# Re-spacing the w_sp sums, adding b_sp on VectorE alone, and one lo part moved ahead at the start, in an FNet and gMLP block on one core

## The chip, the cores and the metric

The kernel runs on one core of a Trainium2 chip. The metric is the device time of one execution in microseconds. The kernel before took 965.06 us (median of 3 runs, 964.96 to 966.77). The profile is that of one further execution.

## The reference

Two layers stand one behind the other, each scaled, shifted and gated by rows of a modulation vector. The first is a Fourier mixing of the sequence, the second a gated MLP whose gate mixes the sequence with w_sp and adds b_sp:

```python
mod = (_silu(c) @ w_mod).reshape(c.shape[0], 6, 1, -1)
sa, ca, ga, sb, cb, gb = (mod[:, i] for i in range(6))
h = _layernorm(x) * (1 + ca) + sa
a, b = h @ dft_hid_re.T, h @ dft_hid_im.T
x = x + ga * (dft_seq_re @ a - dft_seq_im @ b)
h = _layernorm(x) * (1 + cb) + sb
z = _gelu(h @ w_in)                          # 2048 x 1792
z1, z2 = z[..., :896], _layernorm(z[..., 896:])
g = w_sp @ z2 + b_sp[:, None]                # w_sp is 2048 x 2048
x = x + gb * ((z1 * g) @ w_out)
```

The sequence has 2048 rows, the hidden size is 512, all in fp32.

## The kernel before

**Products in three matmuls.** Each fp32 operand is split into a hi part, rounded to fp32r by ScalarE (`ah`, `hh`, `gh`, `bh`), and a lo part, the rest, made by VectorE (`al`, `hl`, `gl`, `bl`). A product is hi x hi, hi x lo and lo x hi (`matmul3`, L95 to L97).

**Chunks.** The program is a long row of chunks of matmuls on TensorE. Chunk n has one 128 x 512 strip as its moving or weight operand, and up to 12 matmuls. Chunks 0 to 127 are the products with the sequence DFT matrices (`gp`, `mm_a`); in between stand the products with the hidden DFT (`yp`, `mm_y`). `N2` = 128 and `N3` = 144 begin the two halves of w_in (`z1p`, `z2p`), `N4` = 160 the product with w_sp (`gw`, `mm_w`), which ends with chunk 271. The tail (`op`) multiplies with w_out.

**Preparing a chunk.** A block of 512 x 512 comes from DRAM into a `stage` tile (two buffers, four DMAs on SyncE's queue, L151 or L157). VectorE transposes it, two chunks at a time, into `t` (`turn_two`, L204 or L210), ScalarE makes `ah`, VectorE makes `al`. `prep(n)` issues al of chunk n+2 (three buffers, so it waits until chunk n-1 is through on TensorE), on even n the pair of chunks n+4 and n+5, and ah of chunk n+3. The turn of a block's second pair frees its stage, and SyncE then loads the block after the next.

**What sets the order.** The order on each engine is that in which the program issues: `at(n, f, ...)` puts a piece of work behind chunk n's matmuls, `run(n)` issues what was put there. Each engine and each DMA queue takes its own work strictly in this order.

**w_sp in seven products.** The product with w_sp is done in quadrants, by a scheme with seven products (`PROD` = 1, 6, 7, 4, 5, 3, 2, of 16 chunks each, beginning at `NB[p]`) instead of eight. Four of them need sums and differences of w_sp's quadrants. These are made ahead: `load_s` loads a unit (two DMAs on SyncE's queue, L602, 1 MB into a tile `sj`), `sum_s` makes two of the four sums, then two more (VectorE, L607 to L612), and each result goes to DRAM by a DMA on GpSimd's queue (L615). Eight units fall in chunks 90 to 122, through two buffers in a pool `spre0` that takes the memory of the pool of the modulation rows (`change_q`, which so has to follow the last use of modulation row 5); eight more units come later.

**Modulation row 5.** `load_mod` loads it, `sum_mod` sums it in four steps on VectorE (L268, L270), `split_mod` splits it, `spread_mod` spreads it by two matmuls.

**The gate.** `keep_w` copies the product's banks out of PSUM into tiles `g` (ScalarE, L672). `add_bs` adds b_sp (L689): on GpSimd for `p` = 4 and 7, on VectorE for 1 and 6. `make_u` multiplies with z1 (VectorE, L698), `add_w` adds later products into g (VectorE, L678).

**The start.** The first four chunks go through L413, with hh and hl of the first four rows of h in turn: all four matmuls of hi x hi, then lo x hi, then hi x lo. `lo_h` makes hl (L394).

Of the kernel before, what the change touches and what calls it, by code (L numbers as in the profile page):

```python
# [10 lines left out]
AF = mybir.ActivationFunctionType  # L11
ALU = mybir.AluOpType
# [7 lines left out]
def fnet_gmlp_kernel(  # L20
# [32 lines left out]
    nc = tc.nc  # L53
# [69 lines left out]
    def at(n, f, *a):  # L123
        fill.setdefault(n, []).append((f, a))
# [14 lines left out]
    N2 = 4 * len(src)  # L139
# [5 lines left out]
    NB = {p: N4 + 4 * NQ * i for i, p in enumerate(PROD)}  # L145
# [31 lines left out]
    def prep(n):  # L177

        if n not in prepared:
            prepared.add(n)  # L180
            prep_lo(n + 2)
            if n % 2 == 0:
                turn_two(n + 4)
            prep_hi(n + 3)

# [9 lines left out]
    def turn_two(n):  # L195

        if n >= NE:
            return
        b, k = divmod(n, 4)
        st = stage[b]  # L200
        t = blocks.tile([P, 2, Q], F32, tag="t", bufs=2, name=f"t{n}")
        T[n], T[n + 1] = t[:, 0, :], t[:, 1, :]
        if n >= N4:
            nc.vector.transpose(t.rearrange("p r (b i) -> p r b i", i=32), st[:, :, :, 16 * k:16 * k + 32])  # L204
        elif n >= N3:
            for m in range(2):
                nc.vector.transpose(T[n + m].rearrange("p (k a i) -> p a k i", k=4, i=32),
                                    st[:, :, 32 * (k + m):32 * (k + m) + 32].rearrange("p (a k) i -> p a k i", k=4))
        else:
            nc.vector.transpose(t.rearrange("p k (b i) -> p k b i", i=32),  # L210
                                st[:, :, 32 * k:32 * k + 64].rearrange("p b (k i) -> p k b i", k=2))
        if k == 2:
            stage.pop(b)
            load(b + 2)

    def prep_hi(n, eng=None):
        if n >= NE:
            return
        AH[n] = blocks.tile([P, Q], F32R, tag="ah", bufs=4, name=f"ah{n}")
        if eng:  # L220
            eng.tensor_scalar(AH[n], T[n], 1.0, None, op0=ALU.mult)
        else:
            nc.scalar.activation(AH[n], T[n], AF.Copy)  # L223

    def prep_lo(n):
        if n >= NE:
            return
        AL[n] = blocks.tile([P, Q], F32R, tag="al", bufs=3, name=f"al{n}")
        nc.vector.tensor_tensor(AL[n], T.pop(n), AH[n].bitcast(F32), op=ALU.subtract)  # L229
# [388 lines left out]
    GW, UT, X2, OP, G, BH, BL = {}, {}, {}, {}, {}, {}, {}  # L618
    wo_hi, wo_lo, wor, Z1T = {}, {}, {}, {}
# [24 lines left out]
    def mm_w(n):  # L644
        i, m = divmod(n - N4, 4 * NQ)
        p, k, r = PROD[i], m // 2, m % 2
        nf = 4 if p in (1, 6, 4, 2) else 3
        fresh = p in (1, 5, 2)
        if k == 0 and fresh:
            for f in range(nf):  # L650
                k_ = 4 * r + f if p == 1 else 3 * r + f if p == 5 else (6, 7, 0, 1, 2, 3, 4, 5)[4 * r + f]
                GW[r, f] = bank(k_, f"gw{p}_{r}_{f}")
        ah, al = AH.pop(n), AL.pop(n)
        for f in range(nf):
            cols = slice(f * P, (f + 1) * P)
            matmul3(GW[r, f], BH[p, k][:, cols], BL[p, k][:, cols], ah, al, fresh and k == 0, k == 7, not fresh)
        if k == 7:
            if p in (1, 6, 7, 4):
                keep_w(p, r)
            elif p != 2:  # L660
                add_w(p, r, range(3))
            else:
                add_w(p, r, range(2 if r == 0 else 0))

    def keep_w(p, r):

        if p in (1, 4):
            G[p, r] = spre[-1].tile([P, 4, Q], F32, tag="sj", bufs=4, name=f"g{p}_{r}")
        else:
            G[p, r] = gpool[0].tile([P, 3, Q], F32, name=f"g{p}_{r}")  # L670
        for f in range(G[p, r].shape[1]):
            nc.scalar.activation(G[p, r][:, f, :], GW[r, f], AF.Copy)  # L672

    def add_w(p, r, fs):

# [9 lines left out]

    def add_bs(p, r, f):
        g = G[p, r][:, f, :]
        eng, b = (nc.vector, r) if p in (1, 6) else (nc.gpsimd, 2 + r)
        eng.tensor_tensor(g, g, wor["bs", b], op=ALU.add)  # L689

    def load_z1(p, r):
        f0, f1 = (0, 4) if p in (1, 4) else (4, NF)
# [100 lines left out]
    load(2)  # L793
    at(0, lo_h, 2)
    at(0, hi_h, 3)
    at(1, lo_h, 3)
    at(0, load_x, 1, range(2, 4))
    at(2, load_row)
# [7 lines left out]
    for s, n in ((4, 4), (5, 4), (6, 6), (7, 6), (8, 10), (9, 10)):  # L806
        m = n + (s == 9)
# [23 lines left out]
    for j, turn, weigh, row, fold, hi in ((0, (25, 26, 27, 28), (29, 29, 30, 30), 26, (34, 34, 35, 36), (38, 35, 36, 37)),  # L831
# [8 lines left out]
        n = weigh[3] + (3 if j == 0 else 1)  # L840
# [4 lines left out]
            at(hi[k], make_ht, j, k)  # L845
            at(hi[k] + 1, make_ht_lo, j, k)
    for j, load_at, n, m, k, plus_one in ((2, 41, 49, 50, 7, False), (4, 52, 56, 58, 7, True),
                                          (3, 60, 65, 66, 7, False), (5, 68, 85, 86, 6, False)):
        at(load_at, load_mod, j)
        at(n, sum_mod, j, [0, 1])  # L850
        at(m, sum_mod, j, [2, 3])
        at(m + 1, split_mod, j)
        at(m + 3, spread_mod, j, k, cpool if j == 5 else htpool, plus_one)
    for t in range(NQ):
        n = 8 * NQ * (t + 1)
        for i in range(4):
            y = N2 - 1 if t == NQ - 1 else (54, 56, 58, 60)[i] if t == 0 else n + (7, 9, 11, 13)[i] if t == 1 else n + 1 + 3 * i
            if i < 2:
                at(y - 4, load_xr, t, i)
            if t == 0:  # L860
                at((41, 42, 43, 45)[i], mm_y, t, i, (0,))
                at((42, 43, 44, 46)[i], keep_y, t, i)
            at(y, mm_y, t, i, (0, 1) if t else (1,))
            if t < NQ - 1:
                at(y + 1, post_y, t, i)
                at(y + 2, norm_y, t, i)
                at(y + 3 if t else 71 + i, post_h, t, i)
                if i < 2:
                    at(y + 2 if t else y + 3, load_xr, t, i + 2)
            else:  # L870
                if i > 1:
                    at(N2 - 0.25, prep, N2 + i - 2)
                at(N2 - 0.25, post_y, t, i)
                at(N2 - 0.25, norm_y, t, i)
                at(N2 - 0.25, post_h, t, i)
                if i < 2:
                    at(N2 - 0.25, load_xr, t, i + 2)
                for k in ((0,), (1,), (2, 3), ())[i]:
                    at(N2 - 0.25, make_wi, 0, k)
                    at(N2 - 0.25, make_wi_lo, 0, k)  # L880
# [25 lines left out]
        hq.close()  # L906
        spre.append(hp.enter_context(pool("spre0")))

    at(90, change_q)
    at(N2 + 3, change_s)  # L910
    for i, u in enumerate((r, g, b) for g in range(2) for b in range(4) for r in range(2)):
        n = 90 + 4 * i if i < 8 else N2 + 6 + 3 * (i - 8)
        at(n, load_s, *u)
        at(n + 3, sum_s, *u, True)
        at(n + 4, sum_s, *u, False)
    for n in range(N2):
        prep(n)
        mm_a(n)
        run(n)
        run(n + 0.5)  # L920
        run(n + 0.75)
# [6 lines left out]
    for n in range(N2, N3):  # L928
        prep(n)
        run(n)  # L930
        two_first(mm_z1, n, n - N2, ND)
# [8 lines left out]
    for i, p in enumerate(PROD):  # L940
        for k in range(8):
            n = NB[p] + 2 * k
# [25 lines left out]
    at(N4 + 4, change_g)  # L968
    at(NB[3] + 1, change_o)
    for r in range(2):  # L970
        for f in range(4):
            at(NB[5] + 2 + 8 * r + 2 * f, add_bs, 4, r, f)
            if f < 3:
                at(NB[4] + 2 + 3 * r + f, add_bs, 7, r, f)
    at(NB[3] + 3, load_z1, 4, 0)
    at(NB[3] + 4, load_z1, 7, 0)
    for f in range(4):
        at(NB[2] + 3 + f, make_u, 4, 0, f)
        if f < 3:
            at(NB[2] + 7 + f, make_u, 7, 0, f)  # L980
    at(NB[2] + 8, load_z1, 4, 1)
    at(NB[2] + 11, load_z1, 7, 1)
    for f in range(NF):
        n = NB[6] + 3 * f
# [2 lines left out]
        at(n - 2, make_wo, f)  # L987
        at(n - 1, make_wo_lo, f)
    order = [(t, i) for t in (2, 3, 0, 1) for i in range(4)]
    later = {0: [(make_u, 4, 1, 0), (make_u, 4, 1, 1), (add_w, 2, 0, [2])],  # L990
             1: [(make_u, 4, 1, 2), (make_u, 4, 1, 3), (add_w, 2, 0, [3]), (load_z1, 1, 0)],
             2: [(make_u, 7, 1, 0), (make_u, 7, 1, 1), (make_u, 7, 1, 2), (load_z1, 6, 0)],
             3: [(add_w, 2, 1, [0, 1])], 4: [(add_w, 2, 1, [2, 3])]}
    for n, p, r in ((3, 1, 0), (5, 6, 0), (7, 1, 1), (9, 6, 1)):
        for f in range(4 if p == 1 else 3):
            later.setdefault(n + f // 2, []).extend([(add_bs, p, r, f), (make_u, p, r, f)])
# [53 lines left out]
```

## Time and profile before

| | us |
|---|---|
| median of 3 runs | 965.06 |
| the profiled execution | 966.28 |
| its span in the trace | 964.5 |
| TensorE busy | 950.2 |
| VectorE busy | 674.4 |
| ScalarE busy | 366.6 |
| GpSimd busy | 188.7 |
| mean granted clock of TensorE | 0.997 |

Times in the trace count from the span's start. A row of the order of time has start, length, engine, line of the kernel, operation, out<-in, shapes and count; what stands in brackets is how long the engine stood idle just before, and for whom. Matmuls overlap, so their pace is read from start to start. A row of waits has the total, how often, and the longest. A row of windows has, for each of TensorE, its weight loads, VectorE, ScalarE and GpSimd, the busy time and the count, then the granted clock, the DMA engines' share and GB/s. SPq, ACTq and POOLq are queues that issue DMAs.

### The profile page before, as it was taken

Reading aid. Unit: us, or ns where it says so; the run is one execution under the profiler, and the core shown is the slowest. Engines: PE = TensorE matmul, PEld = TensorE weight load, DVE = VectorE, ACT = ScalarE, POOL = GpSimd, SP = SyncE. Lnnn points to the kernel's source line nnn. Section 1 sums busy time; section 2 is a strip of 40 time slices with the busy share of each in tenths; the row PEclk is TensorE's granted clock in tenths of the full one; section 3 lists DMA queues with packets and bytes.
Section 4 is the critical chain, followed back from the end, with each engine's and each line's share of the span. In section 5 each row is a group of like instructions: output and inputs, shape, how many; then the busy total and the mean of one; then the engine's idle time right before and its main releaser. Section 6 shows DMA issues by size and latency. Waiting matters only on the chain.

```text
span 964.5 us, 12252 instructions
## 1 busy us (share of the span) xinstructions
PE 950.2 (99%) x4196; PEld 789.6 (82%) x4196; DVE 674.4 (70%) x980; ACT 366.6 (38%) x631; POOL 188.7 (20%) x342
## 2 busy tenths in 40 slices
PE   8999999999999999989999999999999999999998
PEld 5888888888888888768888999888887888888886
DVE  6799857675465768556536477878689688775882
ACT  4684424232222223122433446635544354432221
POOL 1330000222520254113413344200004050000000
PEclk9999999999999999999999999999999999999999
DMA  9996654566455787787398864555555355933541
GB/s 211 219 222 139 118 128 100 150 164 164 131 132 130 200 265 229 234 234 171 129 293 300 296 215 153 135 138 128 138 120 116 90 131 118 217 94 119 194 161 60
DMA packets 249535, 161.27 MB, mean 167 GB/s; under 512 B 130176, under 2 KB 218240, under 8 KB 249344
## 3 DMA queue, kind: packets, MB, share of 16 engines
q1 hardware_dynamic: 236800, 122.72, 52.5%
q0 software_dynamic: 11424, 37.24, 10.7%
q8 instruction: 33, 0.54, 0.2%
q10 hardware_dynamic: 1248, 0.52, 0.2%
q14 instruction: 30, 0.25, 0.1%
HBM read 123.73 MB, written 36.70 MB: 166 GB/s over the span
## 4 chain that ended last, share of the span: by engine, by line
PE 88%; DMA 6%; DVE 3%; SPq 2%; issue 1%; DVEq 0%; ACTq 0%
PE gp L96 10%; PE gp L97 10%; PE gp L95 10%; PE gw L96 9%; PE gw L95 9%; PE gw L97 9%; DMA sj<-in_B_w_sp_dram 4%; PE z2p L96 3%; PE z2p L97 3%; PE z2p L95 3%; PE op L97 3%; PE z1p L96 3%; PE op L96 3%; PE z1p L95 3%; PE yp L96 3%; PE yp L95 3%
## 5 line engine op out<-in xcount | busy, mean ns | idle before, releaser
L223 ACT ACTIVATE ah<-t 128x512 fp32r<-128x512 f32 x271 | 169.5, 628 | 355.7 <-PE gp L97 164.2
L229 DVE TENSOR_TENSOR al<-t,ah 128x512 fp32r<-128x512 f32 x272 | 193.0, 715 | 155.4 <-PE gp L96 54.9
L96 PE MATMUL gp<-al,hh 128*128 128x512 f32 x496 | 194.1, 391 | 4.5 <-DVE al L229 4.4
L97 PE MATMUL gp<-ah,hl 128*128 128x512 f32 x496 | 193.9, 391 | 0.0
L95 PE MATMUL gp<-ah,hh 128*128 128x512 f32 x496 | 193.9, 391 | 0.0
L96 PE MATMUL gw<-al,bh 128*128 128x512 f32 x400 | 155.9, 390 | 1.4 <-DVE al L229 1.4
L95 PE MATMUL gw<-ah,bh 128*128 128x512 f32 x400 | 155.8, 390 | 0.0
L97 PE MATMUL gw<-ah,bl 128*128 128x512 f32 x400 | 155.8, 390 | 0.0
L96 PEld LDWEIGHTS gp<-al,hh 128*128 128x128 f32 x496 | 93.5, 189 | 25.1 <-DVE al L229 5.7
L95 PEld LDWEIGHTS gp<-ah,hh 128*128 128x128 f32 x496 | 93.6, 189 | 19.5
L97 PEld LDWEIGHTS gp<-ah,hl 128*128 128x128 f32 x496 | 93.4, 188 | 19.4
L210 DVE STREAM_TRANSPOSE t<-stage 128x1024 f32<-128x1024 f32 x70 | 86.7, 1239 | 4.3 <-DMA stage<-in_A_dft_seq_re_dram 3.2
L96 PEld LDWEIGHTS gw<-al,bh 128*128 128x128 f32 x400 | 75.1, 188 | 17.3 <-DVE al L229 1.8
L95 PEld LDWEIGHTS gw<-ah,bh 128*128 128x128 f32 x400 | 75.1, 188 | 15.6
L97 PEld LDWEIGHTS gw<-ah,bl 128*128 128x128 f32 x400 | 75.1, 188 | 15.6
L204 DVE STREAM_TRANSPOSE t<-stage 128x1024 f32<-128x1024 f32 x56 | 69.4, 1238 | 0.9 <-DMA stage<-in_B_w_sp_dram 0.9
L615 POOL DMA_DIRECT2D s_d<-sj x64 | 35.3, 551 | 144.6 <-DVE sj L607 109.2
L637 ACT ACTIVATE bh<-z 128x512 fp32r<-128x512 f32 (+1 forms) x56 | 32.8, 586 | 59.8 <-PE gw L96 55.5
L689 POOL TENSOR_TENSOR g<-g,bs 128x512 f32<-128x512 f32 x14 | 22.5, 1644 | 141.1 <-ACT g L672 141.1
L95 PE MATMUL yp<-hth,gh 128*128 128x512 f32 x128 | 49.9, 389 | 0.0
L97 PE MATMUL yp<-hth,gl 128*128 128x512 f32 x128 | 49.9, 389 | 0.0
L96 PE MATMUL yp<-htl,gh 128*128 128x512 f32 x128 | 49.9, 389 | 0.0
(152 smaller groups left out, 1398.4 us busy)
## 6 DMA issues: line engine op xcount, KB each, us to landing
stage<-in_A_dft_seq_im_dram SPq DMA_DIRECT2D x64, 256.0 KB, 5.5
sj<-in_B_w_sp_dram SPq DMA_DIRECT2D x32, 512.0 KB, 7.5
s_d<-sj POOLq DMA_DIRECT2D x64, 256.0 KB, 4.2
stage<-s_d SPq DMA_DIRECT2D x128, 128.0 KB, 2.9
stage<-in_A_dft_seq_re_dram SPq DMA_DIRECT2D x60, 256.0 KB, 5.0
stage<-in_B_w_sp_dram SPq DMA_DIRECT2D x96, 128.0 KB, 3.0
stage<-h_d SPq DMA_DIRECT2D x32, 256.0 KB, 5.3
z_d<-z POOLq DMA_DIRECT2D x28, 256.0 KB, 6.3
```

What stands on the lines that cost most here:

```text
L95: nc.tensor.matmul(acc, ah, bh, start=first, stop=False, skip_group_check=go_on)
L96: nc.tensor.matmul(acc, ah, bl, start=False, stop=False, skip_group_check=go_on)
L97: nc.tensor.matmul(acc, al, bh, start=False, stop=last, skip_group_check=go_on)
L204: nc.vector.transpose(t.rearrange("p r (b i) -> p r b i", i=32), st[:, :, :, 16 * k:16 * k + 32])
L210: nc.vector.transpose(t.rearrange("p k (b i) -> p k b i", i=32), st[:, :, 32 * k:32 * k + 64].rearrange("p b (k i) -> p k b i", k=2))
L223: nc.scalar.activation(AH[n], T[n], AF.Copy)
L229: nc.vector.tensor_tensor(AL[n], T.pop(n), AH[n].bitcast(F32), op=ALU.subtract)
L615: nc.gpsimd.dma_start(s_d[m, r, g][b * P:(b + 1) * P, :], a)
L637: nc.scalar.activation(BH[p, k][:, :w], b_of(p, k), AF.Copy)
L689: eng.tensor_tensor(g, g, wor["bs", b], op=ALU.add)
```

## The change

It does three things; the products and sums that are computed stay the same.

1. The first eight units of w_sp are loaded at chunks 85, 90, ... 120 instead of 90, 94, ... 118, and summed four and five chunks behind their load instead of three and four. For this `change_q` moves from chunk 90 to 84, and the sums of modulation row 5 from 85 and 86 to 79 and 80 (its split and spread follow, from 87 and 89 to 81 and 83).
2. All of b_sp is added by VectorE. For p = 7 the adds stand in p = 5's chunks; for p = 4 they stand right before the product with z1, in p = 2's chunks and in the tail; two of p = 4's copies out of PSUM become adds of b_sp out of PSUM, three chunks later.
3. At the start, the transpose of the second block's first pair is issued behind chunk 0, after the third row's lo part, instead of in `prep(0)`.

```diff
@@ prep
-            if n % 2 == 0:
+            if n % 2 == 0 and n:
                 turn_two(n + 4)
@@ keep_w
-            nc.scalar.activation(G[p, r][:, f, :], GW[r, f], AF.Copy)
+            if (p, r) == (4, 1) and f > 1:
+                at(NB[5] + 2, nc.vector.tensor_tensor, G[p, r][:, f, :], GW[r, f], wor["bs", 3], ALU.add)
+            else:
+                nc.scalar.activation(G[p, r][:, f, :], GW[r, f], AF.Copy)
@@ add_bs
-        eng, b = (nc.vector, r) if p in (1, 6) else (nc.gpsimd, 2 + r)
-        eng.tensor_tensor(g, g, wor["bs", b], op=ALU.add)
+        nc.vector.tensor_tensor(g, g, wor["bs", r if p in (1, 6) else 2 + r], op=ALU.add)
@@ start
     at(0, hi_h, 3)
+    at(0, turn_two, 4)
     at(1, lo_h, 3)
@@ modulation rows
-                                          (3, 60, 65, 66, 7, False), (5, 68, 85, 86, 6, False)):
+                                          (3, 60, 65, 66, 7, False), (5, 68, 79, 80, 6, False)):
@@ w_sp units
-    at(90, change_q)
+    at(84, change_q)
...
-        n = 90 + 4 * i if i < 8 else N2 + 6 + 3 * (i - 8)
+        n = 85 + 5 * i if i < 8 else N2 + 6 + 3 * (i - 8)
         at(n, load_s, *u)
-        at(n + 3, sum_s, *u, True)
-        at(n + 4, sum_s, *u, False)
+        m = n + (4 if i < 8 else 3)
+        at(m, sum_s, *u, True)
+        at(m + 1, sum_s, *u, False)
@@ adds of b_sp
-        for f in range(4):
-            at(NB[5] + 2 + 8 * r + 2 * f, add_bs, 4, r, f)
-            if f < 3:
-                at(NB[4] + 2 + 3 * r + f, add_bs, 7, r, f)
+        for f in range(3):
+            at(NB[5] + 3 + 6 * r + 2 * f, add_bs, 7, r, f)
...
     for f in range(4):
+        at(NB[2] + 3 + f, add_bs, 4, 0, f)
         at(NB[2] + 3 + f, make_u, 4, 0, f)
...
-    later = {0: [(make_u, 4, 1, 0), (make_u, 4, 1, 1), (add_w, 2, 0, [2])],
+    later = {0: [(add_bs, 4, 1, 0), (make_u, 4, 1, 0), (add_bs, 4, 1, 1), (make_u, 4, 1, 1), (add_w, 2, 0, [2])],
```

How the instructions stand is shown at three places. The first is VectorE's row at the start (`al_238` is chunk 2's lo part, `stage_155` the second block, `hl_260` or `hl_258` the lo part of the third row of h), as a piece of the difference, - before and + now:

```order
 L229 TENSOR_TENSOR al_238<-t_218,ah_220 128x512
-L210 STREAM_TRANSPOSE t_240<-stage_155 128x1024
-L394 TENSOR_TENSOR hl_260<-xn_174,hh_222 128x512
-L229 TENSOR_TENSOR al_268<-t_218,ah_242 128x512
-L394 TENSOR_TENSOR hl_284<-xn_176,hh_262 128x512
-L229 TENSOR_TENSOR al_286<-t_240,ah_270 128x512
+L394 TENSOR_TENSOR hl_258<-xn_174,hh_222 128x512
+L210 STREAM_TRANSPOSE t_262<-stage_155 128x1024
+L229 TENSOR_TENSOR al_268<-t_218,ah_240 128x512
+L394 TENSOR_TENSOR hl_284<-xn_176,hh_260 128x512
+L229 TENSOR_TENSOR al_286<-t_262,ah_270 128x512
```

The lo part and the transpose have changed places; the rest stands as it stood.

The second is SyncE's queue around the w_sp units (`stage` a block of the DFT matrices, four DMAs, `sj` a unit's rows, two). Before:

```order
L151 DMA stage_2787<-in_A_dft_seq_re_dram 32x16x128 x4
L602 DMA sj_2810<-in_B_w_sp_dram 128x2x512 x2
L151 DMA stage_2873<-in_A_dft_seq_re_dram 32x16x128 x4
L602 DMA sj_2896<-in_B_w_sp_dram 128x2x512 x2
L151 DMA stage_3004<-in_A_dft_seq_re_dram 32x16x128 x4
L602 DMA sj_3040<-in_B_w_sp_dram 128x2x512 x2
```

And now:

```order
L151 DMA stage_2636<-in_A_dft_seq_im_dram 32x16x128 x4
L602 DMA sj_2714<-in_B_w_sp_dram 128x2x512 x2
L151 DMA stage_2721<-in_A_dft_seq_re_dram 32x16x128 x4
L151 DMA stage_2798<-in_A_dft_seq_re_dram 32x16x128 x4
L602 DMA sj_2821<-in_B_w_sp_dram 128x2x512 x2
L151 DMA stage_2880<-in_A_dft_seq_re_dram 32x16x128 x4
L602 DMA sj_2939<-in_B_w_sp_dram 128x2x512 x2
```

Before, each of the eight units stood right behind a stage; now they are spread over ten stages, and the first unit stands two stages earlier.

The third is VectorE's row in p = 5, NB[5] + 2 to NB[5] + 5 (`gw_1_2` and `gw_1_3` are banks of PSUM, L128 is the line that issues what `at` put there; `g_1_6913` belongs to p = 4, `g_0_6533` to p = 7). Before:

```order
L642 TENSOR_TENSOR bl_3_6988<-z_0_3_4799,bh_3_6962 128x384
L229 TENSOR_TENSOR al_6991<-t_6928,ah_6977 128x512
L229 TENSOR_TENSOR al_7006<-t_6966,ah_6993 128x512
L204 STREAM_TRANSPOSE t_7008<-stage_6873 128x1024
L642 TENSOR_TENSOR bl_4_7021<-z_1_0_4998,bh_4_7004 128x384
L229 TENSOR_TENSOR al_7024<-t_6966,ah_7010 128x512
```

And now:

```order
L642 TENSOR_TENSOR bl_3_6980<-z_0_3_4799,bh_3_6954 128x384
L128 TENSOR_TENSOR g_1_6913<-gw_1_2_5480,bs 128x512
L128 TENSOR_TENSOR g_1_6913<-gw_1_3_5481,bs 128x512
L229 TENSOR_TENSOR al_6984<-t_6920,ah_6969 128x512
L691 TENSOR_TENSOR g_0_6533<-g_0_6533,bs 128x512
L229 TENSOR_TENSOR al_7000<-t_6958,ah_6986 128x512
L204 STREAM_TRANSPOSE t_7002<-stage_6867 128x1024
L642 TENSOR_TENSOR bl_4_7015<-z_1_0_4998,bh_4_6997 128x384
L229 TENSOR_TENSOR al_7017<-t_6958,ah_7004 128x512
L691 TENSOR_TENSOR g_0_6533<-g_0_6533,bs 128x512
```

The adds of b_sp now stand between the lo parts on VectorE; GpSimd's row no longer has any.

## The prediction

> **What bounds the kernel now.** I read the page's busy times first, then TensorE's waits, then the windows of equal length, and last the order of time on the engines around each hole.
>
> ```profile
> PE 950.2 (99%) x4196; PEld 789.6 (82%) x4196; DVE 674.4 (70%) x980; ACT 366.6 (38%) x631; POOL 188.7 (20%) x342
> ```
>
> TensorE is busy 99% of the span, so no change of order can win much: a gain comes only from places where TensorE stands still, or runs slower than its own pace. Who kept it waiting:
>
> ```profile
> PE gp L96 <- DVE al L229: 4.4, 2, 2.9
> ...
> PE gw L96 <- DVE al L229: 1.4, 1, 1.4
> PE gp L413 <- DVE hl L394: 1.1, 1, 1.1
> ```
>
> All three waits are for VectorE's lo parts. The change touches each of the three places. The windows put the first at 400 to 432 us; in every other window from 32 to 944, but for that of 720, TensorE was busy 16.00 of 16:
>
> ```profile
> 400.00:416.00 16.00, 14.47 (x63) 11.36 (x62) 7.35 (x11) 3.24 (x6) 2.16 (x4) 1.00 0.81 242
> 416.00:432.00 16.00, 13.06 (x51) 10.33 (x50) 9.19 (x12) 2.41 (x4) 3.24 (x6) 0.89 0.77 226
> ```
>
> The second window also holds the only drop of the granted clock behind the start, to 0.89. TensorE's rows there (each the first of a stretch, start and length in us):
>
> ```profile
> 406.29 0.39 PE L95 MATMUL gp<-ah,hh 128*128 128x512 f32 x1
> ...
> 419.29 0.39 PE L95 MATMUL gp<-ah,hh 128*128 128x512 f32 x1
> 422.61 0.50 PE L96 MATMUL gp<-al,hh 128*128 128x512 f32 x1 [2.94 <-DVE al L229]
> ...
> 423.66 0.63 PE L97 MATMUL gp<-ah,hl 128*128 128x512 f32 x1
> ...
> 427.05 0.39 PE L96 MATMUL gp<-al,hh 128*128 128x512 f32 x1
> ...
> 429.55 0.39 PE L95 MATMUL gp<-ah,hh 128*128 128x512 f32 x1
> ```
>
> From 427.05 to 429.55 lie 11 matmuls: 0.227 us each, 2.73 for a chunk of 12. From 406.29 (chunk 120) to 429.55 (chunk 126) lie 72, which at that pace take 16.36 us; they took 23.26. So **6.90 us** are lost here. 3.09 of it is the step from 419.29 to 422.61, and the 8 matmuls from 423.66 to 427.05 take 3.39 instead of 1.82, which is the half clock behind that wait, 1.57.
>
> **Part 1: w_sp every fifth chunk.** Why al was late is seen on VectorE and SyncE:
>
> ```profile
> 352.08 2.07 SPq L602 DMA_DIRECT2D sj<-in_B_w_sp_dram  x2
> ...
> 363.16 0.69 DVE L607 TENSOR_TENSOR sj<-sj 128x512 f32<-128x512 f32 x1 [2.38 <-DMA sj<-in_B_w_sp_dram]
> ...
> 392.61 0.69 DVE L607 TENSOR_TENSOR sj<-sj 128x512 f32<-128x512 f32 x1 [3.88 <-DMA sj<-in_B_w_sp_dram]
> ...
> 395.81 1.91 SPq L151 DMA_DIRECT2D stage<-in_A_dft_seq_im_dram  x4
> 397.90 1.73 SPq L602 DMA_DIRECT2D sj<-in_B_w_sp_dram  x2
> ...
> 406.09 0.69 DVE L607 TENSOR_TENSOR sj<-sj 128x512 f32<-128x512 f32 x1 [6.08 <-DMA sj<-in_B_w_sp_dram]
> ...
> 420.53 0.69 DVE L607 TENSOR_TENSOR sj<-sj 128x512 f32<-128x512 f32 x1 [7.04 <-DMA sj<-in_B_w_sp_dram]
> ```
>
> The units run in a ring: a sum waits at the head of VectorE's queue for its rows; behind it stand al and the transpose that frees the stage; SyncE issues the stage's four DMAs, and only then the next rows. Landing took 8.19 us (397.90 to 406.09), the whole ring 13.48 (392.61 to 406.09) and 14.44. Four chunks last 10.9 us, so each unit comes some 2.6 us later than the one before it. Its leeway: loaded in chunk n and summed in chunk n+3, it must begin before al of chunk n+6 is due, 6 x 2.73 + 0.23 - 0.7 - 1.35 = 14.6 us after chunk n began (al and two sums in front). It comes at about 0.6 + 1.24 + 1.9 + 8.2 = 12.0 (al, transpose, stage issues, landing). Leeway 2.6; the three units behind the last yp block (chunks 110, 114, 118) lose 3 x 2.6 = 7.8; 7.8 - 2.6 = 5.2, and the waits seen are 6.90 - 1.57 = 5.3. The account closes, which is why I trust it.
>
> After the change a unit has five chunks, 13.64 us, against a ring of 13.48, and one chunk more until its sum: the limit is 17.3 us after chunk n. With the longest landing of the trace, 11.08 us (352.08 to 363.16), it comes at 14.9. So 2.4 us remain in the worst case and nothing adds up. In most units the ring is even open: SyncE has the rows ahead of the next stage and not behind it. I take the whole 6.90, half clock included. The bounds: 0 won, if landing and not spacing sets the ring, to 6.90. The moved DMAs are the same in number (two loads on SyncE, four sums on VectorE, four stores on GpSimd's queue each unit); the last unit now ends in chunk 125, in front of the weights' load, which waits for TensorE's last gp matmul anyway.
>
> The buffer of the rows needs the sixth mod row summed earlier, in chunks 79 and 80, where VectorE also makes the four gl. Rows of that place, the sums' where they stand now:
>
> ```profile
> 276.72 0.68 DVE L229 TENSOR_TENSOR al<-t,ah 128x512 fp32r<-128x512 f32 x1
> ...
> 279.05 0.68 DVE L229 TENSOR_TENSOR al<-t,ah 128x512 fp32r<-128x512 f32 x1
> ...
> 280.71 0.39 PE L95 MATMUL gp<-ah,hh 128*128 128x512 f32 x1
> ...
> 289.52 0.48 DVE L268 TENSOR_SCALAR wm<-wm,sc 128x512 f32<-128x512 f32 x1
> ...
> 293.41 1.50 DVE L270 SCALAR_TENSOR_TENSOR wm<-wm,sc 128x512 f32<-128x512 f32 x2
> ```
>
> The al of 276.72 (chunk 82) gets 0.48 + 0.75 in front of it, that of 279.05 (chunk 83) 1.23 + 1.50 in all: it ends at 279.73 + 2.73 = 282.46. Chunk 82 starts at 280.71, so chunk 83 wants it at 280.71 + 2.73 + 0.23 = 283.67. 1.2 us remain: cost 0. Without that cover it costs what is missing. The pair of matmuls that spreads the row only moves from behind chunk 89 to behind chunk 83.
>
> **Part 2: b_sp without GpSimd.** The second hole lies in chunk 209 (733.16 to 737.55: 4.39 us for 12 matmuls, so **1.66** lost):
>
> ```profile
> 733.16 0.39 PE L95 MATMUL gw<-ah,bh 128*128 128x512 f32 x1
> ...
> 737.55 0.39 PE L95 MATMUL gw<-ah,bh 128*128 128x512 f32 x1
> ...
> 724.09 0.65 DVE L642 TENSOR_TENSOR bl<-z,bh 128x512 fp32r<-128x512 f32 x1
> ...
> 725.85 1.29 DVE L229 TENSOR_TENSOR al<-t,ah 128x512 fp32r<-128x512 f32 x2
> ...
> 728.22 1.68 DVE L642 TENSOR_TENSOR bl<-z,bh 128x512 fp32r<-128x512 f32 x1
> ...
> 733.08 3.46 DVE L229 TENSOR_TENSOR al<-t,ah 128x512 fp32r<-128x512 f32 x2
> ...
> 728.05 9.65 POOL L689 TENSOR_TENSOR g<-g,bs 128x512 f32<-128x512 f32 x6 [107.00 <-ACT g L672]
> L689 DVE TENSOR_TENSOR g<-g,bs x14: 680/684/685, 902.3 to 934.3; 128x512 f32<-128x512 f32 x14
> ```
>
> While GpSimd adds (728.05 to 737.7), VectorE's bl takes 1.68 instead of 0.65, and from bl to al pass 4.86 us instead of 1.76. Without these adds, al starts at 728.22 + 1.76 = 729.98 and ends near 730.7; TensorE wants it at 733.39. 2.7 us remain, so the 1.66 go whole. GpSimd loses 14 adds, ScalarE two copies. VectorE gains 12 adds of 0.68, and two that take b_sp to gw out of PSUM. No row shows these; the nearest, L678, adds gw to g:
>
> ```profile
> 838.64 1.84 DVE L678 TENSOR_TENSOR g<-gw,g 128x512 f32<-128x512 f32 x3
> ```
>
> That is 0.61 each, so they lie between 0.61 and 0.68. Six adds stand in every other chunk of p=5, the two from PSUM in one of its chunks, four beside the products with z1, two in the tail. What hides them: VectorE is 70% busy, and makes al two chunks ahead. Cost 0; if nothing hid them, 14 x 0.68 = 9.5 us at most.
>
> **Part 3: third row's lo part first.** The start:
>
> ```profile
> 15.82 1.20 PE L413 MATMUL gp<-ah,hh 128*128 128x512 f32 x4 [0.38 <-ACT hh L389]
> 16.85 1.08 PE L413 MATMUL gp<-al,hh 128*128 128x512 f32 x4
> ...
> 20.04 1.07 PE L413 MATMUL gp<-ah,hh 128*128 128x512 f32 x4
> ...
> 15.85 0.65 DVE L229 TENSOR_TENSOR al<-t,ah 128x512 fp32r<-128x512 f32 x1
> 17.14 1.25 DVE L210 STREAM_TRANSPOSE t<-stage 128x1024 f32<-128x1024 f32 x1 [0.63 <-DMA stage<-in_A_dft_seq_im_dram]
> 18.30 0.65 DVE L394 TENSOR_TENSOR hl<-xn,hh 128x512 fp32r<-128x512 f32 x1
> ...
> 17.92 0.61 ACT L389 ACTIVATE hh<-xn 128x512 fp32r<-128x512 f32 x1
> ```
>
> hl waited behind a transpose that itself waited for its block. Put ahead, it runs in the idle 0.63 us, from 16.45 to 17.10; TensorE wants it at 16.85 + 0.91 = 17.76. Chunk 2 then takes 2.73 + 0.12 (the slower first group) instead of 4.22: **1.37** won. Next late is hh of the fourth row, 18.53, against 18.67: 0.14 to spare. The transpose still begins at 17.14, when its block lands, so nothing behind it moves.
>
> **Sum.** 6.90 + 1.66 + 1.37 = 9.93. The profiled execution took 966.28 us, 1.78 around its span of 964.5, and stands 1.22 over the median of 965.06. 966.28 - 9.93 = 956.35; on the median's footing 955.1.
>
> The idle of 2.94 us was followed by half clock, the other of 4.4 - 2.9 = 1.5 was not. [...]
>
> **Rivals.**
> - One w_sp sum still comes late, since five chunks bunch the loads with the stages in another way. For: the ring has only 0.16 us to spare where a stage stands in front (chunks 90 and 110). Against: 2.4 us of leeway at the longest landing. Price: a wait like the last one, 3.09, with or without its half clock: 958.2 to 959.8.
> - Half clock has another cause and stays, with 1.57: 956.7. Against: it stands nowhere but behind the long wait.
> - The start is held by the DMA: the transpose at 17.14 waited 0.63 us for its block already, and a later block may be as late for an earlier TensorE. No gain there, 956.5.
> - The spacing does not do what it says: the ring stretches with it, 6.90 stay: 965.06 - 3.03 = 962.0. Against: the landing of 8 us is the same at several loads.
> - Slower: landing gets longer than 8.3 us in every unit, since more stages share the queues, and the ring is over 13.64 again. With landing L, three units lose 3 x (L - 8.3) - 2.4, and each wait over some 3 us another 1.57. At L = 13 that is 11.7 + 4.7 = 16.4 instead of 6.90; less 3.03 won, 971.5. It decides from about L = 11.4, where 6.9 + 3.1 of half clock eat all 9.93; the trace shows one landing of 11.08, beside many near 8.
>
> **Chances.** Forecast 0.70 (955.1, itself 954.2 to 957); one late sum 0.12; half clock stays 0.03; start held 0.05; spacing without effect 0.06; slower 0.02; no change by things I do not see 0.02. The range 954.2 to 959.0 holds the forecast, the half clock, the start and most of the late sum, some 0.85; its low end is the forecast less 0.9, the spread of single runs. Faster by over 0.2% (1.9 us, about what a measurement of this kernel can tell) 0.96, within 0.02, slower 0.02.
>
> **What would show it.** Right: no TensorE wait at L96 for al in gp or gw; granted clock 1.00 from 400 to 432; the sums of sj no longer waiting 6 to 7 us for their rows; no GpSimd work from 700 to 850, and bl near 0.65 throughout; hl at 16.4 on VectorE. Wrong: a wait of TensorE at chunks 80 to 84, 95 to 98 or 116 to 127, a new one in p=5 or p=2, or an early gain that is gone again before chunk 16.

## The result and the profile after

The changed kernel takes **956.52 us** (median of 4 runs, 955.97 to 957.61); the kernel before, run beside it, took 965.40 (964.96 to 966.77). The ratio is 0.9907 (95% interval 0.989 to 0.9924), so it is some 0.9% faster. The profiled execution took 956.76 us, its span is 955.0 and the mean granted clock 1.00. The forecast was 955.1, with a range of 954.2 to 959.0.

The page's busy times after:

```profile
PE 947.7 (99%) x4196; PEld 788.4 (83%) x4196; DVE 674.2 (71%) x994; ACT 366.2 (38%) x629; POOL 166.8 (17%) x328
```

VectorE has 14 instructions more and is not busy for longer (674.2 against 674.4): GpSimd works 21.9 us less, and the operations beside its adds are short again (bl 0.65 us, where it took 1.68). TensorE's waits after, all that are left:

```profile
PE busyp L310 <- DVE busy L250: 1.5, 1, 1.5
PE gp L413 <- DVE ah L221: 1.4, 1, 1.4
PE gp L413 <- ACT hh L389: 0.6, 2, 0.4
```

None is for `al` any more, nor for `hl`; all three belong to the start. The windows where the holes were, with the columns as before:

```profile
400.00:416.00 16.00, 16.00 (x72) 13.26 (x71) 10.15 (x13) 3.80 (x6) 3.25 (x6) 1.00 0.94 298
416.00:432.00 16.00, 16.00 (x72) 13.25 (x71) 10.28 (x14) 4.92 (x8) 2.18 (x4) 1.00 1.00 235
720.00:736.00 16.00, 16.00 (x73) 13.23 (x72) 13.54 (x21) 7.92 (x15) 0.00 (x0) 1.00 0.58 132
```

TensorE is busy 16.00 of 16 in each, the granted clock is 1.00, and GpSimd does nothing in the third. The DMA engines are busy 0.94 and 1.00 of the time in the first two, where before they were busy 0.81 and 0.77, and that costs TensorE nothing.

**Where the time went** is read from the starts of some matmuls: the first of chunks 4 and 100, of z1p (chunk 128), of p = 4 (chunk 208) and of p = 5 (chunk 224), then the last one of all. Order of time, before:

```profile
22.77 0.39 PE L95 MATMUL gp<-ah,hh 128*128 128x512 f32 x1
...
335.57 0.39 PE L95 MATMUL gp<-ah,hh 128*128 128x512 f32 x1
...
456.75 0.39 PE L95 MATMUL z1p<-ah,wih 128*128 128x512 f32 x1
...
960.36 0.39 PE L97 MATMUL op<-woh,ul 128*128 128x512 f32 x1
```

And after:

```profile
15.71 1.19 PE L413 MATMUL gp<-ah,hh 128*128 128x512 f32 x4 [0.38 <-ACT hh L389]
...
21.85 0.39 PE L95 MATMUL gp<-ah,hh 128*128 128x512 f32 x1
...
334.65 0.39 PE L95 MATMUL gp<-ah,hh 128*128 128x512 f32 x1
...
950.83 0.39 PE L97 MATMUL op<-woh,ul 128*128 128x512 f32 x1
```

With the other edges taken from the trace in the same way (z1p begins at 448.89 after; p = 4 lasts from 730.44 to 775.63 before, from 722.58 to 766.10 after), the whole program splits like this:

| stretch | before | after | won | forecast |
|---|---|---|---|---|
| chunks 2 and 3 (from 15.82, 15.71) | 6.95 | 6.14 | 0.81 | 1.37 |
| chunks 4 to 99 | 312.80 | 312.80 | 0.00 | 0 |
| chunks 100 to 127 | 121.18 | 114.24 | 6.94 | 6.90 |
| chunks 128 to 207 | 273.69 | 273.69 | 0.00 | 0 |
| p = 4, chunks 208 to 223 | 45.19 | 43.52 | 1.67 | 1.66 |
| from chunk 224 to the last matmul | 184.73 | 184.73 | 0.00 | 0 |

Everything that was not meant to change is the same to a hundredth of a microsecond. Parts 1 and 2 are as forecast; the start gave 0.81 where 1.37 was put. In the experiments below, "the stretch" of a part means one of these rows. It is a sharper measure than the time of an execution, since chunk 2 itself begins between 14.7 and 16.0 us in these traces, whatever the edit.

### The profile page after: what moved, and what is told of

Its sections match the earlier page's. It is cut to its first block, busy times and chain, and to the rows that moved or that the text cites. A ratio compares the mean times of both kernels' runs of the same rounds, so it can differ in the third digit from the quotient of the medians.

```text
span 955.0 us, 12241 instructions
## 1 busy us (share of the span) xinstructions
PE 947.7 (99%) x4196; PEld 788.4 (83%) x4196; DVE 674.2 (71%) x994; ACT 366.2 (38%) x629; POOL 166.8 (17%) x328
## 4 chain that ended last, share of the span: by engine, by line
PE 98%; DMA 1%; DVE 1%; issue 0%; ACT 0%; POOL 0%; ACTq 0%; DVEq 0%
PE gp L95 12%; PE gp L96 12%; PE gp L97 12%; PE gw L95 10%; PE gw L97 9%; PE gw L96 9%; PE yp L96 3%; PE yp L95 3%; PE yp L97 3%; PE z2p L96 3%; PE z2p L95 3%; PE z2p L97 3%; PE op L97 3%; PE z1p L95 3%; PE op L95 3%; PE z1p L96 3%
## 5 line engine op out<-in xcount | busy, mean ns | idle before, releaser
L229 DVE TENSOR_TENSOR al<-t,ah 128x512 fp32r<-128x512 f32 x272 | 185.8, 686 | 167.0 <-PE gp L96 65.4
L96 PE MATMUL z2p<-wil,ah 128*128 128x448 f32 x128 | 46.7, 365 | 0.0
```

What stands on the lines that cost most here:

```text
L96: nc.tensor.matmul(acc, ah, bl, start=False, stop=False, skip_group_check=go_on)
```

## The experiments

Each kernel is the changed one with the edit shown. The median of the kernel before was 965.05 us beside the first four, 966.07 beside the next four, 965.45 beside the ninth and tenth, and the one run beside the last two took 965.30.

| run | median us | ratio to before (95%) | chunks 2, 3 | 100 to 127 | p = 4 |
|---|---|---|---|---|---|
| changed kernel | 956.52 | 0.9907 (0.989 to 0.9924) | 6.14 | 114.24 | 43.52 |
| e1_units_undone | 963.83 | 0.9988 (0.9978 to 0.9997) | 6.18 | 121.63 | 43.52 |
| e2_bsp_undone | 957.86 | 0.9929 (0.9914 to 0.9944) | 6.17 | 114.24 | 45.16 |
| e3_lead_only | 956.09 | 0.9914 (0.9898 to 0.9931) | 6.13 | 114.24 | 43.52 |
| e4_spacing_only | 956.60 | 0.9913 (0.9899 to 0.9928) | 6.13 | 114.24 | 43.52 |
| e5_bsp_old_place | 956.73 | 0.9909 (0.9889 to 0.9929) | 6.18 | 114.24 | 43.52 |
| e6_bsp_pool_late | 958.16 | 0.9923 (0.9907 to 0.9939) | 6.14 | 114.24 | 45.16 |
| e7_start_undone | 957.13 | 0.9912 (0.9896 to 0.9928) | 7.22 | 114.24 | 43.52 |
| e8_shift_on_dve | 955.69 | 0.9897 (0.9878 to 0.9916) | 5.62 | 114.24 | 43.52 |
| e9_rows_on_act | 956.65 | 0.9906 (0.9884 to 0.9928) | 6.48 | 114.24 | 43.52 |
| e10_p4_on_pool | 956.44 | 0.9906 (0.9887 to 0.9926) | 6.13 | 114.24 | 43.52 |
| e11_fill_one (1 run) | 955.94 | | 5.73 | 114.24 | 43.52 |
| e12_fill_two (1 run) | 956.32 | | 6.15 | 114.24 | 43.52 |

Of the other stretches, chunks 4 to 99 took up to 0.23 us longer in e4, e9 and e11 (313.03, 312.99 and 312.93); the rest are the same in every trace.

### Each part undone alone: e1, e2, e7

w_sp's units as before:

```diff
-    (5, 68, 79, 80, 6, False)
+    (5, 68, 85, 86, 6, False)
-    at(84, change_q)
+    at(90, change_q)
-        n = 85 + 5 * i if i < 8 else N2 + 6 + 3 * (i - 8)
+        n = 90 + 4 * i if i < 8 else N2 + 6 + 3 * (i - 8)
-        m = n + (4 if i < 8 else 3)
+        m = n + 3
```

> The changed kernel with the w_sp units, row 5's sums and the pool where they stood before (load at 90 + 4i, sums 3 and 4 chunks behind). My account: the 6.9 us come back, so some 963.4 us against 956.5, with TensorE waiting about 1.6 us in chunk 120 and 3.1 in chunk 124 for al, and half clock behind the second. Rival (the wait was shared with the other parts, or came from the phase of the DMAs): clearly less than 6.9, or a wait elsewhere.

The waits for al are back, and the kernel is only 0.12% faster than before. The order of time on TensorE around them:

```profile
408.36 0.54 PE L96 MATMUL gp<-al,hh 128*128 128x512 f32 x1 [2.32 <-DVE al L229]
408.69 0.63 PE L97 MATMUL gp<-ah,hl 128*128 128x512 f32 x1
...
412.10 0.40 PE L96 MATMUL gp<-al,hh 128*128 128x512 f32 x1
...
423.62 0.50 PE L96 MATMUL gp<-al,hh 128*128 128x512 f32 x1 [2.49 <-DVE al L229]
423.95 0.39 PE L97 MATMUL gp<-ah,hl 128*128 128x512 f32 x1
```

Two waits of 2.32 and 2.49 us stand here where one of 2.94 and one of 1.5 stood before, and half clock (matmuls of 0.63 instead of 0.39, some 0.43 us apart) follows the first, shorter one, not the second. The expectation had 1.6 and then 3.1, with half clock behind the second: the total was right, its division was not. The stretch takes 7.39 us more than in the changed kernel. So part 1 is worth its 7 us by itself.

All of b_sp for p = 4 and 7 on GpSimd again, at its old places (`add_bs`, `keep_w` and the four lists of adds as in the kernel before):

```diff
-        nc.vector.tensor_tensor(g, g, wor["bs", r if p in (1, 6) else 2 + r], op=ALU.add)
+        eng, b = (nc.vector, r) if p in (1, 6) else (nc.gpsimd, 2 + r)
+        eng.tensor_tensor(g, g, wor["bs", b], op=ALU.add)
```

> The changed kernel with b_sp of p=4 and p=7 added by GpSimd again, at the old places. My account: 1.66 us come back, some 958.2 us, as one TensorE wait of about 1.35 us in chunk 209, with VectorE's al and bl near 1.7 us while GpSimd adds. Rival (the wait had gone anyway, since the earlier part of the program runs differently): no wait, 956.5.

One wait is back, and its stretch takes 1.64 us longer. The second fence is the order of time around it:

```profile
PE gw L96 <- DVE al L229: 1.3, 1, 1.3
```

```profile
719.24 9.64 POOL L689 TENSOR_TENSOR g<-g,bs 128x512 f32<-128x512 f32 x6 [106.94 <-ACT g L672]
719.40 1.67 DVE L642 TENSOR_TENSOR bl<-z,bh 128x512 fp32r<-128x512 f32 x1
...
724.26 3.46 DVE L229 TENSOR_TENSOR al<-t,ah 128x512 fp32r<-128x512 f32 x2
```

In the changed kernel the same operations, not beside GpSimd's, take 0.65 and 0.65:

```profile
720.36 0.65 DVE L642 TENSOR_TENSOR bl<-z,bh 128x512 fp32r<-128x512 f32 x1
...
722.12 1.29 DVE L229 TENSOR_TENSOR al<-t,ah 128x512 fp32r<-128x512 f32 x2
```

The transpose at the start ahead of hl again:

```diff
-            if n % 2 == 0 and n:
+            if n % 2 == 0:
-    at(0, turn_two, 4)
```

> The changed kernel with the second block's first transpose ahead of the third row's lo part again. Of the two profiles: chunks 2 and 3 take 6.95 us instead of 6.14, so 0.8 us come back, 957.3; GpSimd's last small instruction of the fourth row (L352) takes 0.6 us again and not 1.1, and hh of the fourth row ends some 0.4 us earlier. Rival (hh's delay is chance of the run): hh ends where it ends in the changed kernel, and 1.4 us come back.

Chunks 2 and 3 take 7.22 us, 1.08 more than in the changed kernel: between the expectation (0.8) and its rival (1.4). TensorE's wait for hl is back, and GpSimd's L352 (the fourth row's shift, 128x1) takes 0.59 us, as in the kernel before:

```profile
15.63 0.59 POOL L352 TENSOR_SCALAR first<-first 128x1 f32<-128x1 f32 x1
...
18.87 1.19 PE L413 MATMUL gp<-ah,hl 128*128 128x512 f32 x4 [1.35 <-DVE hl L394]
```

The 0.27 us above the 6.95 of the kernel before come from the second block: its transpose waits 0.91 us for it here and 0.63 there, and begins 1.59 and 1.32 us behind the start of chunk 2. So part 3 is worth 0.8 or 1.1 us, by the two traces without it. This rests on the traces: the single runs of e7 (956.74 to 957.53) and of the changed kernel (955.97 to 957.61) overlap.

### What in part 1 did it: e3, e4, e9

Part 1 changed two things: five chunks between units instead of four, and four chunks from a load to its first sum instead of three. First the longer lead alone, every fourth chunk as before:

```diff
-        n = 85 + 5 * i if i < 8 else N2 + 6 + 3 * (i - 8)
+        n = 90 + 4 * i if i < 8 else N2 + 6 + 3 * (i - 8)
```

(with `change_q` and modulation row 5 back at 90, 85 and 86)

> The changed kernel with spacing 4 again (load at 90 + 4i, row 5 summed at 85 and 86), but sums 4 and 5 chunks behind the load. The ring as the prediction put it (a period of 10.9 us against a ring of 13.5): each unit is still 2.6 us later than the one before, with leeway 5.3: 7.8 - 5.3 = 2.5 us of waiting for al near chunk 124, some 959.0 us. Rival (place in the queue: at 4 chunks behind, the sum stands behind the transpose that frees the next stage, so SyncE no longer waits for the sum and the ring is open): no TensorE wait, 956.5. Second rival (the DMA engines cannot carry a unit in 10.9 us): landing over 10 us, and waits as before, up to 963.

Then the spacing alone:

```diff
-        m = n + (4 if i < 8 else 3)
+        m = n + 3
```

> The changed kernel with spacing 5 but sums 3 and 4 chunks behind the load, as before. The ring (13.5 us against 13.64): nothing adds up, at most one landing of 11 us costs 0.3 us: 956.5 to 956.9. Rival (the lead of the sum is what did it): the waits of before stay, 959 to 963.

Neither has a wait of TensorE for al, and in both the stretch takes 114.24 us. Here my account fell: by it, a ring of 13.48 us cannot run every 10.9 us, whatever the lead, and e3 does just that, as the first rival of its expectation said. What differs is how long VectorE stood at the head of its queue for rows. The line, for 300 to 440 us and so for the first eight units, says who kept the first add of a sum (L607) waiting, the total in us and how often; in the kernel before, in the changed kernel, in e1, e3 and e4, in this order:

```profile
  DMA sj<-in_B_w_sp_dram: 28.0, 7
```

```profile
  DMA sj<-in_B_w_sp_dram: 1.2, 3
```

```profile
  DMA sj<-in_B_w_sp_dram: 31.3, 7
```

```profile
  DMA sj<-in_B_w_sp_dram: 2.1, 2
```

```profile
  DMA sj<-in_B_w_sp_dram: 9.7, 3
```

In e3 a sum stands one chunk later on VectorE, and that is behind the transpose that frees the stage which SyncE loads ahead of the next rows:

```profile
389.00 1.24 DVE L210 STREAM_TRANSPOSE t<-stage 128x1024 f32<-128x1024 f32 x1
390.17 0.65 DVE L607 TENSOR_TENSOR sj<-sj 128x512 f32<-128x512 f32 x1
390.27 1.92 SPq L151 DMA_DIRECT2D stage<-in_A_dft_seq_im_dram  x4
...
392.36 1.50 SPq L602 DMA_DIRECT2D sj<-in_B_w_sp_dram  x2
```

In the kernel before, the sum at 392.61 came first and the transpose behind it, at 394.55. In e3 the sum no longer holds up that transpose, so the chain from a sum to the next rows is cut, and 13.48 us is no longer a period. In e4 the chain stands, but has time; sums wait 9.7 us in all, and al has enough lead to bear it.

A direct trial of that chain: e1's spacing and lead, and only the rows' DMAs on another queue, where no stage stands ahead of them.

```diff
-            nc.sync.dma_start(SJ[r, g, b][:, 2 * i:2 * i + 2],
+            (nc.scalar if g == 0 else nc.sync).dma_start(SJ[r, g, b][:, 2 * i:2 * i + 2],
```

(beside e1's edit)

> The kernel of after with w_sp's units back at every fourth chunk and summed three and four chunks behind their load, as before, but the rows of the first eight units are loaded by DMAs on ScalarE's queue instead of SyncE's. Theory (a ring through SyncE's queue: sum, transpose, stage's DMAs, rows, landing, sum): on ScalarE's queue the rows wait for no stage, so the lateness is not handed from unit to unit; no wait of TensorE for al over 0.3 us between 300 and 440 us, granted clock 1.00 there, and the time as that of after, 955.7 to 957.3 us; the sums of sj wait under 4 us each. Rival A (three chunks between load and sum are too few whatever the queue): the two waits of 2.3 to 2.5 us stay, 962 to 964 us. Rival B (issuing holds ScalarE, ah comes late instead): waits of TensorE for ah, L221, near chunks 90 to 118, 1 us or more in all.

The stretch takes 114.24 us again, without a longer lead and without more spacing. The sums' wait for rows shrinks from 31.3 us in e1 to 6.4 (one more wait, 1.6, is put down to a store, `s_d<-sj`):

```profile
  DMA sj<-in_B_w_sp_dram: 6.4, 3
```

So the queue was the link: rows waiting behind a stage's DMAs, which waited for a transpose, which waited behind a sum. Chunks 2 and 3 take 0.34 us longer here than in the changed kernel, though no row is loaded there. VectorE's transpose at 13.82 waited 0.31 us for its block in this execution, and al and L352 behind it are as much later; so this is one execution's start and not the edit. Rival B, ah late by 1 us or more, did not show.

### What in part 2 did it: e5, e6, e10

p = 7's six adds on VectorE, but at the places that they had on GpSimd:

```diff
-            at(NB[5] + 3 + 6 * r + 2 * f, add_bs, 7, r, f)
+            at(NB[4] + 2 + 3 * r + f, add_bs, 7, r, f)
```

> The changed kernel with the six adds of p=7 back in chunks 210 to 215 (p=4's first chunks), but on VectorE. GpSimd's adds as the cause: no TensorE wait in chunk 209, 956.5 us, VectorE's al at 0.69. Rival (too much work for VectorE at that place, whoever adds): the six adds of 0.68 us meet pairs of chunks in which VectorE has 4.2 of 5.4 us of work already, and TensorE waits again, up to 1.7 us: 958.2.

No wait for al, 43.52 us: at the old place the adds cost nothing on VectorE either. It is the engine that mattered. Then the other way round, at the new places on GpSimd:

```diff
-        nc.vector.tensor_tensor(g, g, wor["bs", r if p in (1, 6) else 2 + r], op=ALU.add)
+        eng = nc.gpsimd if p == 7 else nc.vector
+        eng.tensor_tensor(g, g, wor["bs", r if p in (1, 6) else 2 + r], op=ALU.add)
```

> The changed kernel with the six adds of p=7 on GpSimd, at the new places in p=5 (chunks 227 to 237, one in every other chunk). My account: each slows VectorE's two-input work near it to about 1.7 us, but only one or two instructions each, and the lead of al covers it: no TensorE wait, 956.5. Rival (any add on GpSimd costs TensorE): six times about 1 us spread over p=5, up to 6 us: 957 to 962.

This expectation missed: the wait of 1.3 us is back, in the same chunk. GpSimd's row tells why:

```profile
720.48 9.65 POOL L692 TENSOR_TENSOR g<-g,bs 128x512 f32<-128x512 f32 x6 [106.92 <-ACT g L675]
```

GpSimd had stood idle for 106.92 us, and took the adds as soon as ScalarE had copied their operands, 54 us ahead of the time when VectorE makes the first of them in the changed kernel (774.2). The later place in the program did not delay GpSimd, since its queue was empty.

p = 4's eight adds back on GpSimd (and its two copies back on ScalarE), p = 7's six on VectorE:

```diff
+        eng = nc.gpsimd if p == 4 else nc.vector
+        eng.tensor_tensor(g, g, wor["bs", r if p in (1, 6) else 2 + r], op=ALU.add)
...
+        for f in range(4):
+            at(NB[5] + 2 + 8 * r + 2 * f, add_bs, 4, r, f)
```

> The kernel of after with p = 4's eight adds of b_sp back on GpSimd (and its two copies back on ScalarE); p = 7's six stay on VectorE. Theory (only the adds at 728 us met a lo part that was due): no wait of TensorE for al in gw, 955.7 to 957.3 us, although VectorE's two-input operations during GpSimd's 12.9 us of adds take 1.6 us and more instead of 0.65. Rival (any adds on GpSimd in p = 5 make al late): a wait of 1 us or more near 771 to 785 us, 957.5 to 958.5 us.

956.44 us and no wait. VectorE is busy all the time beside those adds, and TensorE does not notice; in the window of 768 to 776, where GpSimd adds for 6.48 us:

```profile
768.00:776.00 8.00, 8.00 (x37) 6.63 (x36) 8.00 (x8) 3.33 (x6) 6.48 (x4) 1.00 0.24 54
```

So the six adds of p = 7 bring the whole 1.67 us. Moving p = 4's eight, two of which now read PSUM, won nothing and cost nothing.

### Where part 3 lost 0.56 us: e8, e11, e12

After the change, the order of time at the start, on VectorE, GpSimd, ScalarE and TensorE:

```profile
15.74 0.65 DVE L229 TENSOR_TENSOR al<-t,ah 128x512 fp32r<-128x512 f32 x1
15.94 1.11 POOL L352 TENSOR_SCALAR first<-first 128x1 f32<-128x1 f32 x1
16.32 0.68 DVE L394 TENSOR_TENSOR hl<-xn,hh 128x512 fp32r<-128x512 f32 x1
...
17.08 0.81 ACT L119 ACTIVATE xn<-x,first 128x511 f32<-128x511 f32 x1 [1.42 <-POOL first L352]
...
17.66 1.07 PE L413 MATMUL gp<-ah,hl 128*128 128x512 f32 x4
...
18.32 0.61 ACT L389 ACTIVATE hh<-xn 128x512 fp32r<-128x512 f32 x1
...
18.99 1.20 PE L413 MATMUL gp<-ah,hh 128*128 128x512 f32 x4 [0.26 <-ACT hh L389]
```

hl runs at 16.32, as forecast, and TensorE no longer waits for it. But L352 now takes 1.11 us and ends at 17.05, just when hl ends (17.00); the fourth row's xn, hh and chunk 3 follow it. In the kernel before, with VectorE idle behind al, it took 0.60 and ended 0.14 behind al's end (15.85 + 0.65). The traces of the other kernels repeat this: 1.11 in each of the eight that also have hl right behind al (e1 to e6, e9, e10), 0.59 in e7. The order of time before:

```profile
16.04 0.60 POOL L352 TENSOR_SCALAR first<-first 128x1 f32<-128x1 f32 x1
16.67 0.82 ACT L119 ACTIVATE xn<-x,first 128x511 f32<-128x511 f32 x1 [0.91 <-POOL first L352]
```

First the shift on VectorE, behind chunk 2's al and ahead of hl, then xn:

```diff
             prep_lo(n + 2)
+            if n == 0:
+                shift_first(3, nc.vector)
+                norm_x(3)
...
-        nc.gpsimd.tensor_scalar(mv[:, 3:4], mv[:, 0:1], mv[:, 2:3], -1.0, op0=ALU.mult, op1=ALU.mult)
+        if s < 3:
+            shift_first(s, nc.gpsimd)
```

> The changed kernel with the fourth row's shift (-mean/std, L352, 128x1) on VectorE, right behind chunk 2's al, instead of on GpSimd. If VectorE's two-input lo part holds GpSimd's small instruction, and with it ScalarE's xn and hh: xn of the fourth row starts near 16.6 instead of 17.1, hh ends near 18.0, TensorE does not wait for it, and chunk 3 starts 0.4 to 0.55 us earlier: 956.0. Rival (xn or hh is held by something else, or hl, now 0.2 us later, becomes the wait): no gain, 956.5.

```profile
15.72 0.20 DVE L364 TENSOR_SCALAR first<-first 128x1 f32<-128x1 f32 x1
...
15.96 0.82 ACT L119 ACTIVATE xn<-x,first 128x511 f32<-128x511 f32 x1 [0.89 <-DVE first L364]
...
18.00 1.09 PE L424 MATMUL gp<-ah,hh 128*128 128x512 f32 x4
```

Chunk 3 waits for nothing, and chunks 2 and 3 take 5.62 us: 1.33 less than in the kernel before. That is what part 3 was forecast to bring. Its median, 955.69 us, is the lowest of the study, but the interval of its ratio overlaps that of the changed kernel; it is the stretch that tells the two apart.

Is L352 held by hl, or by VectorE being busy at all? One more operation ahead of hl, a transpose with one input (e11), or an add of two (e12), neither with any use:

```diff
+    at(0, filler)
     at(0, lo_h, 2)
```

```diff
+        nc.vector.transpose(junk, h_hi[0].rearrange("p a b -> p (a b)").bitcast(F32))
```

```diff
+        nc.vector.tensor_tensor(junk, h_hi[0].rearrange("p a b -> p (a b)").bitcast(F32), h_hi[1].rearrange("p a b -> p (a b)").bitcast(F32), op=ALU.add)
```

> The kernel of after with one more operation on VectorE ahead of the third row's hl: a transpose of 128x512, which reads one operand and writes a tile that nobody uses. Counted from the start of al (L229) in chunk 2. Theory (a two-input operation of VectorE holds GpSimd's small L352 until it ends; one with a single input doesn't): L352 takes 0.5 to 0.7 us as in the kernel before, though VectorE is as busy; the fourth row's xn starts 0.8 us behind that al and not 1.34 us, and TensorE has no wait for hh in chunk 3, though hl itself comes 0.6 to 0.7 us later. Rival (any work of VectorE holds it, or L352's length has another cause): L352 takes 1.1 us or more, xn starts 1.3 us or later, and the wait for hh stays at 0.26 us or grows.

> The kernel of after with one more operation on VectorE ahead of the third row's hl: an add of two 128x512 operands into a tile that nobody uses, so that al, this add and hl stand one behind the other. Counted from the start of al (L229) in chunk 2. Theory (L352 is held as long as two-input operations of VectorE follow each other): L352 takes 1.5 to 1.9 us, the fourth row's xn starts 1.8 to 2.1 us behind that al, and TensorE waits 0.7 to 1.0 us for hh in chunk 3. Rival (GpSimd gets its turn between two such operations): L352 takes 0.5 to 1.2 us, xn starts at most 1.4 us behind al, and the wait for hh is 0.3 us or less.

With the transpose (L393), al itself at 15.20:

```profile
15.39 0.60 POOL L352 TENSOR_SCALAR first<-first 128x1 f32<-128x1 f32 x1
15.77 0.70 DVE L393 STREAM_TRANSPOSE junk<-hh 128x512 f32<-128x512 f32 x1
16.02 0.81 ACT L119 ACTIVATE xn<-x,first 128x511 f32<-128x511 f32 x1 [0.91 <-POOL first L352]
...
18.14 1.09 PE L417 MATMUL gp<-ah,hh 128*128 128x512 f32 x4
```

With the add of two, al at 15.29:

```profile
15.47 1.11 POOL L352 TENSOR_SCALAR first<-first 128x1 f32<-128x1 f32 x1
15.86 0.68 DVE L393 TENSOR_TENSOR junk<-hh,hh 128x512 f32<-128x512 f32 x1
...
16.46 0.68 DVE L398 TENSOR_TENSOR hl<-xn,hh 128x512 fp32r<-128x512 f32 x1
16.62 0.81 ACT L119 ACTIVATE xn<-x,first 128x511 f32<-128x511 f32 x1 [1.42 <-POOL first L352]
```

VectorE is as busy in e11 as in e12, yet L352 takes 0.60 behind the transpose and 1.11 beside the add. xn starts 0.82 and 1.33 us behind al. So it is VectorE's operations with two inputs that hold it, by one trace of each. In e12 L352 ends at 16.58, when the add ends (16.54), and not behind hl, which had begun by then: of e12's two readings the second held, GpSimd gets its turn between two such operations. Though e11 does more work than the changed kernel, and its hl comes later, its chunks 2 and 3 take 5.73 us, 0.41 less.

## Why the prediction was nearly right

- **What bounds the kernel.** Right. TensorE was busy 99% of the span before and is so after, and the whole gain lies at the three places where it had stood still.
- **Part 1, 6.90 us.** The size was right (6.94), the half clock included. That does not speak for the account, since 6.90 was all that was lost there, and any cure brings it. The account was right in its links (e9) and wrong in its condition. "After the change a unit has five chunks, 13.64 us, against a ring of 13.48" takes the ring as given and the spacing as the cure. e3 shows that four chunks do, once the sum stands behind the transpose that frees the next stage. So the changed kernel has two cures where one is enough, and its sums wait 1.2 us in all.
- **The sixth modulation row at 79 and 80**, forecast at 0 with 1.2 us to spare: chunks 4 to 99 take 312.80 us in both kernels. Right.
- **Part 2, 1.66 us.** Right in size (1.67), place and engine. The 14 adds on VectorE were put between 0.61 and 0.68 us each; all took 0.68, those that read PSUM too. They are all hidden, as said.
- **Part 3, 1.37 us, gave 0.81.** The step that failed reads "Next late is hh of the fourth row, 18.53, against 18.67: 0.14 to spare ... nothing behind it moves". hh did move: it ended at 18.93, since L352 was held while hl ran. Chunk 3 began 0.43 us later for it, and its first matmuls, behind a wait again, took the other 0.13. Moving a VectorE operation in time moved a GpSimd operation that no queue and no semaphore ties to it. The profile before held the hint: L352 took 0.60 us there, and 0.27 in the rows ahead of it, for the same 128x1 shape. With L352 on VectorE, part 3 gives 1.33 (e8).
- **The sum and its footing.** On the profiled execution the forecast was 956.35 and the measurement 956.76: 0.56 missing from part 3, less 0.05 more from parts 1 and 2 and some 0.1 from an earlier chunk 2. On the median, 955.1 against 956.52. Another 0.98 of that is the footing, by which the forecast went from a profiled execution to a median: the profiled execution before stood 1.22 over its median, the one after only 0.24 over its own, and taking 1.22 off both was not founded.
- **Half clock.** It went with the wait, as the row of 2.94 us had it. The slower rival's "over some 3 us" for such a wait was not shown: e1 has half clock behind a wait of 2.32.
- **The rivals.** No sum comes late, the start is not held by its DMA (the transpose begins at 16.91 and waits for nothing), and no landing grew long enough to matter. The spacing does do what it says (e4), though it is not the only thing that does.

## What to carry to other kernels

When a transfer is late by more with each round, look for the ring that goes through a queue, and find the one link that can be cut: a consumer put behind the operation that frees the next buffer, or the transfer on a queue of its own, can do as much as more time per round (114.24 us for the stretch in e3, e9 and e4 alike). An operation moved into an idle gap of VectorE need not be free if GpSimd works in that gap, even if GpSimd's operation is as small as L352 (128x1, 1.11 us beside hl instead of 0.60); look what stands beside it on both engines. An engine with an empty queue can run ahead of the place that the program gives its work: in e6 GpSimd's adds began 54 us ahead of it, so moving them later moved nothing.

## What the runs showed of the hardware

**VectorE's operations with two inputs and GpSimd's take longer beside each other.** Beside GpSimd's adds (1.64 us each on average) VectorE's operations with two inputs of 128x512 mostly take 1.66 to 1.78 us instead of 0.65, its transposes of 128x1024 still 1.23. The other way, a 128x1 operation of GpSimd that takes 0.27 us in the third row, mostly beside a transpose, took 1.11 beside two operations with two inputs in a row. In e12, with the add behind al, it took 1.11 again, and in e11, with the transpose behind al, 0.60. In the two cases of 1.11 it ended with the second of the two operations: 17.05 against 17.00 in the changed kernel, 16.58 against 16.54 in e12. Why L352, starting while al ran, let one more operation pass ahead of it, no run here tells.

**Half clock followed waits of 2.94 and 2.32 us, and not waits of 1.49 and 2.49.** In the kernel before, the granted clock was 0.50 for 3.413 us (423.61 to 427.02), behind the wait of 2.94 that ended at 422.61; the wait of 1.49, ended at 408.17, had no half clock behind it. In e1 the slow matmuls last 3.41 us (408.69 to 412.10), behind the wait of 2.32, ended at 408.36; none are behind the wait of 2.49, ended at 423.62. So the length of the wait alone did not decide it. Full clock lasted 416.43 us ahead of the half clock of the kernel before and 535.89 behind it, and 948.91 in the changed kernel, which is 122, 157 and 278 times 3.4133.

An estimate from these three stretches, that the clock changes only at steps of 3.413 us, fits the four waits. Counted back from where half clock began, e1's first wait lies in the one step from 405.28 to 408.69. Counted on, an edge falls at 422.34, and cuts the second wait into 1.21 and 1.28. Before, 2.4 of the 2.94 us lie in the step from 420.20 to 423.61, and the wait of 1.49 lies whole in the one from 406.54 to 409.96. By this estimate, 2.3 us of idleness in one step were enough, 1.5 were not, and 2.49 across two were not. That the idleness within one step decides is an inference from these four waits, and was not tried by itself.
